# Four edits to a hand-made planner: shorter keep-up products, another issuer for one copy, a longer order search, another load order

## The chip, the cores and the metric

The kernel runs on one core of one Trainium2 chip. A core has TensorE (PE) for matrix products, VectorE (DVE), ScalarE (ACT), GpSimd (POOL) and SyncE (SP), which here only issues transfers. Each engine carries out its own list of instructions in order and waits on semaphores for the others; transfers run on 16 DMA engines. The metric is the device time in microseconds of one execution.

## The reference

Blocked attention, then a layer of two matrix products with a gated softmax between them. The shapes are B=4, H=8, S=768, D=64; x has 3072 rows of 512; w_in is 512x1024, w_out 1024x512; all float32.

```
k_sum = k.reshape(B,H,24,32,D).max(axis=3)        # one key for each block of 32
v_sum = v.reshape(B,H,24,32,D).mean(axis=3)       # one value for each block
scores = [ scale*q@k.T where |i-j| < 16, else -1e9  |  scale*q@k_sum.T + log(32) ]
a   = softmax(scores);   attn = a @ [v | v_sum];   x = attn as rows of H*D
h   = x @ w_in
solu = h * softmax(h)
ln  = (solu - mean)/sqrt(var + 1e-6) * g_ln
out = ln @ w_out
```

## The kernel before

Rows of x are cut in 24 tiles t of 128. Each batch has 768 rows, in three groups g of 256 rows, and each group has two tiles. The window of 16 neighbours is taken by loading, for each 64 queries, the 96 keys and values around them (WIN); 24 block keys or block means follow, 120 columns in all (KC).

The work of a step, by the names of the profile:

- `scores` (L578): products of keys and queries into `s`. VectorE adds the mask and takes the row minimum of the negated score (L597), ScalarE takes exponentials (L605), and the sum's reciprocal scales them (L611, then L288/L289 on `e`).
- `values_turn` (L633, tile `t`): the weights are transposed on TensorE and copied by ScalarE or VectorE to `at` (L281 is the copy helper's ScalarE line, L282 VectorE's, L283 GpSimd's).
- `values` (L672, tile `x`): products with the values `vt`. Its copies are split in a high and a low part, `xh` and `xl` (L678), since each product with weights is made of three passes of reduced precision.
- `first(t)` (L697, tile `h`): 24 products with w_in. Then follow the maximum (L707), the exponential (L712), the product with h (L720) and the normalization (L723 to L745).
- `turn(t)` (L633, tile `lt`) and `second(t)` (L775, tile `o`): the transposed rows, 24 products with w_out; ScalarE scales and stores (L780, L784).
- weights arrive as 64-bit integers that hold float64 (`raw`, L356) and are rounded by shifts and masks on ScalarE, VectorE and GpSimd into a high and a low part (`rounded`, L368 to L388, then L281, L288/L289 or L400, L402); w_in comes in eight pieces of 512 KB, w_out in eight.

Block means of v: for batch 0 TensorE sums the rows `st_v` (three loads, L447, "r" in the load string) with a selector matrix (L459), and ScalarE copies the result to `vsum` (L463). The mean rows must stand below the window rows of every tile `vt`: `load_v2` (L541) copies them there with a transfer, after the tile's own load (`load_v`, L535). For the very first tile they are multiplied apart (L664). Batch 1's means are made the same way (L472) and brought to `vsum`, of which there is a single buffer, by four small transfers on ScalarE's queue (L485); batches 2 and 3 use GpSimd's sums (L501).

No order is written down. Every operation is declared with the engines that can do it, a cost for each, and what it reads and writes. `Plan.order` simulates the engines with these costs and gives every free engine the ready operation with the smallest due time; an operation that can run on several engines goes where it is cheapest then. `Plan.issue` computes due times, runs `order` with random noise added to them 64 times, keeps the order with the earliest planned end of TensorE's work, and emits the instructions in that order. So the lists of all engines, SyncE's loads included, follow the plan; SyncE's due time is its place in the program, plus the noise. The string LOADS gives the places of the first loads: k is a pair of heads' keys (400 KB), q half of the first queries (256 KB), w a piece of w_in (512 KB), r rows of v (512 KB), v the first tile of values (1024 KB), Q and V the second group's.

In gaps that the plan leaves on TensorE up to FILL = 80 us, `keep_up` puts products of zeros (L900) into a tile that is overwritten later, to keep TensorE's clock up; each counts as 0.22 us in the plan.

Of the kernel before, what the change touches and what calls it, by code (L numbers as in the profile page):

```python
# [43 lines left out]
WPT = 2  # L44


LOADS = "wwkwqkkkqwwwrrrwwvQV"
NEG = -8.0e9
SCALE = 1.0 / math.sqrt(D)

# [22 lines left out]
class Plan:  # L73
# [8 lines left out]
    START = 0.7  # L82
    COLD, FILL = 6.9, 80.0
    IDLE = 0.22
    WAIT, FAR = 1.5, 200
    DEAR = {"dve": 1.0, "act": 0.3, "pool": 1.0}
    SYNC = 0.13
    TRIES, NOISE = 64, 3.0

    def __init__(self):  # L90
        self.ops, self.rings, self.banks, self.idle = [], {}, {}, None
# [15 lines left out]
    def op(self, engine, cost, fn, r=(), w=(), nbytes=0, after=(), alt=(), port=False):  # L107

        deps = set(after)

        def of(table, part):
            for k, v in table.items():
                if part is None or k is None or k == part:
                    deps.update(v)

        o = Op({e: (c, f) for e, c, f in ((engine, cost, fn), *alt)}, deps,
               len(self.ops), nbytes, port)
        r = [x if isinstance(x, tuple) else (x, None) for x in r]  # L120
        w = [x if isinstance(x, tuple) else (x, None) for x in w]
        for b, part in r:
            of(b.writers, part)
        for b, part in w:
            of(b.writers, part)
            of(b.readers, part)
            for p in b.prev:
                deps.update(p.ops)
                p.gone = True
        assert not any(b.gone for b, _ in r + w)  # L130
        for b, part in r:
            b.readers.setdefault(part, []).append(o)
            b.ops.append(o)
        for b, part in w:
            b.writers.setdefault(part, []).append(o)
            b.ops.append(o)
        deps.discard(o)
        self.ops.append(o)
        return o

    def issue(self):

        for o in self.ops:
            for d in o.deps:
                d.users.append(o)
        for o in reversed(self.ops):
            o.due = min([u.due for u in o.users] + ([o.prio] if "pe" in o.can else []), default=o.prio)
            if "sp" in o.can:
                o.due = o.prio
        due, best = [o.due for o in self.ops], None  # L150
        for seed in range(self.TRIES):
            noise = random.Random(seed)
            for o, x in zip(self.ops, due):
                o.due = x + (noise.gauss(0.0, self.NOISE) if seed else 0.0)
            order = self.order()
            if order:
                end = max(o.end for o in order if "pe" in o.can)
                if best is None or end < best[0]:
                    best = end, order, [(o.start, o.end, o.engine, o.cost, o.fn) for o in self.ops]
        _, order, kept = best  # L160
        for o, x in zip(self.ops, kept):
            o.start, o.end, o.engine, o.cost, o.fn = x
        at, done = self.START, set()
        for o in order:
            if o.engine == "pe":
                while at + self.SYNC < min(o.start, self.FILL):
                    at += self.keep_up(at, done)
                at = max(at, o.start) + o.cost * (2 if o.start < self.COLD else 1)
            done.add(o)
            o.fn()  # L170
# [72 lines left out]
    def keep_up(self, at, done):  # L243


        for tag in "hxs":
            b = next((b for b in self.rings[tag] if b.ops[0] not in done), None)
            if b and all(o in done and o.end + self.SYNC < at for p in b.prev for o in p.ops):
                self.idle(b.ap)
                return self.IDLE * (2 if at < self.COLD else 1)  # L250
        return 0.1
# [3 lines left out]
def attn_then_solu(ctx: ExitStack, tc: tile.TileContext, q, k, v, vr, vb, w_in, w_out, g_ln, out):  # L255
# [3 lines left out]
    nc = tc.nc  # L259
    plan = Plan()  # L260
    op = plan.op
    pe, act, dve, pool, sp = "pe", "act", "dve", "pool", "sp"
# [274 lines left out]

    def load_v2(b, g):
        x, y = vt[b, g], vsum[b]
        e, cost, queue = (sp, 0.43, nc.sync) if b else (act, 0.8, nc.scalar)  # L540
        return op(e, cost, lambda: queue.dma_start(  # L541
            out=x.ap[WIN:KC], in_=y.ap[WIN:KC, :].rearrange("p (o c) -> p o c", o=1).broadcast_to([NB, G, DM])),
            r=[y], w=[(x, 1)], nbytes=NB * 8192)
# [254 lines left out]
    }  # L798
    for x in LOADS:
        first_loads[x].pop(0)()  # L800
# [8 lines left out]
    for i in range(2 * NKC):  # L809
        split_w_in(*divmod(i, 2))  # L810
        if i % 2 == 0 and i < 2 * NPP:
            run(values_turn(0, 0, i // 2))
            run(values(0, 0, i // 2, 0, True))

    begun = [load_v2(*its[1])]
    for i in range(3):
        load_v_rows(1, i)
# [20 lines left out]
    for t in range(NT):  # L838
        n, j = divmod(t, 2)
        b, g = its[n]  # L840
# [47 lines left out]
        if j == 1 and n + 2 < len(its):  # L888
            load_v2(*its[n + 2])
# [54 lines left out]
```

## Time and profile before

| | |
|---|---|
| median of 3 runs | 397.38 us (397.09 to 397.52) |
| profiled execution | 397.45 us |
| its span, first to last instruction | 395.7 us |
| mean granted TensorE clock | 0.999 |
| busy: PE, DVE, ACT, POOL | 386.6, 275.4, 248.7, 97.9 us |
| moved by transfers | 49.24 MB |

The span is what the views below divide up; 1.75 us of the execution's own time lie outside it. In a row of the timeline or of the chain of waits the first number is the start and the second the length. "SPq" and "ACTq" are instructions by which SyncE and ScalarE issue a transfer. Products on TensorE are pipelined and their ends are modelled, so that busy rows overlap. What stands in brackets at the end is idle time before the row and what ended it.

### The profile page before, as it was taken

What the parts mean: (1) busy time and instruction counts of PE and PEld (TensorE: products, weight loads), DVE (VectorE), ACT (ScalarE), POOL (GpSimd) and SP (SyncE); (2) the same over time, 40 slices, a digit from 0 to 9 for tenths busy, and PEclk for the clock granted to TensorE, in tenths of its full rate; (3) what the DMA queues carried; (4) which work ended last, traced back from release to release, by engine and by line L of the source; (5) the groups of instructions that cost most, each with busy time, mean ns of one, the idle gap of its engine ahead of it and who ended that gap; (6) DMA issues with size and microseconds to landing.
All of it is one profiled execution on the core that took longest, in us unless ns stands there. A gap on an engine that the chain in (4) does not pass through costs nothing.

```text
span 395.7 us, 9677 instructions
## 1 busy us (share of the span) xinstructions
PE 386.6 (98%) x3697; PEld 298.3 (75%) x3703; DVE 275.4 (70%) x884; ACT 248.7 (63%) x746; POOL 97.9 (25%) x245
## 2 busy tenths in 40 slices
PE   8999998999999999999999999999999999999996
PEld 3436766677878888878888888878888887878776
DVE  4999998999789866577767657657657654554330
ACT  3889686999798756658558466468466463533411
POOL 4224010416837221236220121221021021101100
PEclk9999999999999999999999999999999999999999
DMA  7999992136277320463330410430310000000011
GB/s 287 411 410 369 409 329 78 56 113 185 70 248 208 113 103 0 141 175 104 123 112 2 150 66 27 156 73 28 108 48 27 2 28 27 16 12 28 27 55 53
DMA packets 14994, 49.24 MB, mean 124 GB/s; under 512 B 1836, under 2 KB 2092, under 8 KB 13412
## 3 DMA queue, kind: packets, MB, share of 16 engines
q1 hardware_dynamic: 11084, 41.89, 30.8%
q10 hardware_dynamic: 3864, 6.74, 4.7%
q8 instruction: 29, 0.48, 0.5%
q14 instruction: 17, 0.14, 0.1%
HBM read 40.11 MB, written 6.29 MB: 117 GB/s over the span
## 4 chain that ended last, share of the span: by engine, by line
PE 85%; DMA 6%; ACT 3%; DVE 2%; issue 1%; ACTq 1%; SPq 1%; DVEq 0%
PE o L775 35%; PE h L697 30%; PE x L672 6%; PE s L578 5%; PE t L633 3%; PE lt L633 3%; DMA st_v<-in_vr 3%; DMA raw<-in_w_in 2%; DMA vt<-vsum 2%; PE vs_ps L459 1%; PE x L900 1%; ACT he L712 1%; DVE he L720 1%; ACT at L281 1%; PE x L664 1%
## 5 line engine op out<-in xcount | busy, mean ns | idle before, releaser
L775 PE MATMUL o<-w,lh 128*128 128x512 f32 (+1 forms) x400 | 128.0, 390 | 0.1
L697 PE MATMUL h<-w,xh 128*128 128x512 f32 x384 | 127.0, 398 | 0.4 <-DVE he L720 0.4
L605 ACT ACTIVATE e<-e,nm 128x120 f32<-128x120 f32 x192 | 73.1, 385 | 25.0 <-DVE nm L597 25.0
L775 PEld LDWEIGHTS o<-w,lh 128*128 128x128 f32 x400 | 74.1, 188 | 18.5 <-issue 2.4
L697 PEld LDWEIGHTS h<-w,xh 128*128 128x128 f32 x384 | 72.1, 188 | 18.9 <-ACT e L605 0.8
L775 PE MATMUL o<-w,ll 128*128 128x512 f32 (+1 forms) x200 | 76.9, 384 | 0.0
L697 PE MATMUL h<-w,xl 128*128 128x512 f32 x192 | 75.6, 394 | 0.0
L707 DVE TENSOR_REDUCE hm<-h 128x1 f32<-128x512 f32 x48 | 32.6, 686 | 42.7 <-PE h L697 42.7
L281 ACT COPY at<-t 120x512 f32<-120x512 f32 x46 | 24.8, 587 | 46.1 <-PE t L633 45.6
L775 PEld LDWEIGHTS o<-w,ll 128*128 128x128 f32 x200 | 37.6, 188 | 6.6
L697 PEld LDWEIGHTS h<-w,xl 128*128 128x128 f32 x192 | 36.1, 188 | 7.5
L597 DVE CUSTOM_DVE_ANT_0 e<-s,mask 128x120 f32<-128x120 f32 x192 | 40.6, 276 | 1.3 <-PE s L578 1.3
L712 ACT ACTIVATE he<-h,hm 128x512 f32<-128x512 f32 x48 | 32.8, 697 | 9.4 <-DVE hm L709 9.4
L605 ACT ACTIVATION_READ_ACCUMULATOR e<-e,nm 128x1 f32 x192 | 36.5, 190 | 0.0
L760 DVE TENSOR_TENSOR ll<-lt,lh 128x512 fp32r<-128x512 f32 x48 | 31.9, 682 | 6.0 <-ACT lh L281 5.8
L739 POOL TENSOR_SCALAR ss<-ss 128x1 f32<-128x1 f32 x24 | 7.1, 297 | 115.0 <-ACT sq L735 114.9
L720 DVE SCALAR_TENSOR_TENSOR he<-h,hz,he 128x512 f32<-128x512 f32 x48 | 34.1, 746 | 0.4
L672 PE MATMUL x<-at,vt 120*64 120x64 f32 (+1 forms) x768 | 28.3, 225 | 1.5 <-ACT at L281 1.5
L672 PEld LDWEIGHTS x<-at,vt 120*64 120x64 f32 (+1 forms) x768 | 24.6, 138 | 6.3 <-ACT at L281 2.8
L288 DVE TENSOR_TENSOR e<-e,z 128x960 f32<-128x960 f32 x23 | 26.6, 1156 | 0.5
L281 ACT CAST lh<-lt 128x512 fp32r<-128x512 f32 x33 | 18.6, 596 | 12.9 <-PE lt L633 10.0
L735 ACT ACTIVATE sq<-he 128x1024 bf16<-128x1024 f32 x24 | 25.2, 1050 | 0.2
(94 smaller groups left out, 499.6 us busy)
## 6 DMA issues: line engine op xcount, KB each, us to landing
vt<-in_v SPq DMA_DIRECT2D x12, 1024.0 KB, 5.4
kraw<-in_k SPq DMA_DIRECT2D x16, 400.0 KB, 9.1
out<-os ACTq DMA_DIRECT2D x23, 256.0 KB, 2.0
qt<-in_q SPq DMA_DIRECT2D x11, 512.0 KB, 5.5
raw<-in_w_in SPq DMA_DIRECT2D x8, 512.0 KB, 10.7
raw<-in_w_out SPq DMA_DIRECT2D x8, 512.0 KB, 9.5
st_v<-in_vr SPq DMA_DIRECT2D x6, 512.0 KB, 12.5
st_v<-in_vb SPq DMA_DIRECT2D x8, 384.0 KB, 3.3
```

What stands on the lines that cost most here:

```text
L281: by = {act: lambda: nc.scalar.copy(out=to(), in_=of()), dve: lambda: nc.vector.tensor_copy(out=to(), in_=of()), pool: lambda: nc.gpsimd.t ...
L288: by = {dve: lambda: nc.vector.tensor_tensor(out=to(), in0=a(), in1=b(), op=kind), pool: lambda: nc.gpsimd.tensor_tensor(out=to(), in0=a() ...
L597: nc.vector.tensor_tensor_reduce(out=e.ap[:, n, :], in0=sc.ap[:, j, (2 * i + up) * KC:(2 * i + up + 1) * KC], in1=mask[:, mi, :], scale=-S ...
L605: nc.scalar.activation(out=e.ap[:, n, :], in_=e.ap[:, n, :], func=AF.Exp, bias=nm.ap[:, n:n + 1], scale=-1.0, accum_out=z.ap[:, n:n + 1])
L672: nc.tensor.matmul(xp()[j * D:(j + 1) * D, i, qs], vs.ap[:k, u, cs], at.ap[:k, u % 2, n[j] + u // 2, :], start=not apart, stop=not apart o ...
L697: nc.tensor.matmul(hp.ap, a.ap[:, c, ts], w.ap[:, i], start=(c == 0 and n == 0), stop=(c == NKC - 1 and n == 2))
L707: op(dve, 0.6, lambda i=i, hp=hp: nc.vector.tensor_reduce(out=nms.ap[:, i:i + 1], in_=hp.ap, op=ALU.max, axis=AX.X, negate=True), r=[hp], ...
L712: op(act, 0.71, lambda i=i, hp=hp: nc.scalar.activation(out=part(i), in_=hp.ap, func=AF.Exp, bias=nm.ap, accum_out=zs.ap[:, i:i + 1]), r=[ ...
L720: op(dve, 0.67, lambda i=i, hp=hp: nc.vector.scalar_tensor_tensor(out=part(i), in0=hp.ap, scalar=zs.ap[:, 0:1], in1=part(i), op0=ALU.mult, ...
L735: op(act, 1.13, lambda: nc.scalar.activation(out=sq.ap, in_=e.ap, func=AF.Square, accum_out=ss.ap), r=[e], w=[sq, ss])
L760: op(dve, 0.6, lambda part=part, r=r: nc.vector.tensor_tensor(out=part(lo), in0=tp.ap[:, r], in1=part(hi).bitcast(F32), op=ALU.subtract), ...
L775: nc.tensor.matmul(o.ap[:, cols], a.ap[:, f, :], w.ap[:, i, cols], start=(f == 0 and n == 0), stop=(f == NFC - 1 and n == 2))
```

## The change

Four parts. The gap in front of a product is filled with zero products only to 0.6 us ahead of its planned start (EASE). The copy of the means for the third group of batch 0, tile (0, 2), is issued by SyncE, where ScalarE issued it; the second group's stays on ScalarE. The search makes 500 tries. The first 16 are as before, with noise of 10 where it was 3; each later one takes the noises of the best try so far and adds new noise to about two in a hundred operations. A try is kept when the planned end of TensorE's work plus half the mean end of its operations isn't later. And the load string is another.

```
-LOADS = "wwkwqkkkqwwwrrrwwvQV"
+LOADS = "wkwqkkwkqwwrwrrwwvQV"
...
+    EASE = 0.6
...
-    TRIES, NOISE = 64, 3.0
+    TRIES, NOISE = 500, 10.0
+    FIRST, FEW = 16, 0.02
...
-        due, best = [o.due for o in self.ops], None
-        for seed in range(self.TRIES):
-            noise = random.Random(seed)
-            for o, x in zip(self.ops, due):
-                o.due = x + (noise.gauss(0.0, self.NOISE) if seed else 0.0)
+        due, best, rnd = [o.due for o in self.ops], None, random.Random(0)
+        for i in range(self.TRIES):
+
+            noise = [x + (rnd.gauss(0.0, self.NOISE) if i < self.FIRST or rnd.random() < self.FEW else 0.0) * (i > 0)
+                     for x in (best[3] if i >= self.FIRST else [0.0] * len(due))]
+            for o, x, n in zip(self.ops, due, noise):
+                o.due = x + n
             order = self.order()
             if order:
-                end = max(o.end for o in order if "pe" in o.can)
-                if best is None or end < best[0]:
-                    best = end, order, [(o.start, o.end, o.engine, o.cost, o.fn) for o in self.ops]
-        _, order, kept = best
+                ends = [o.end for o in order if "pe" in o.can]
+                end = max(ends) + 0.5 * sum(ends) / len(ends)
+                if best is None or end <= best[0]:
+                    best = end, order, [(o.start, o.end, o.engine, o.cost, o.fn) for o in self.ops], noise
+        _, order, kept, _ = best
...
-                while at + self.SYNC < min(o.start, self.FILL):
+                while at + self.SYNC + self.EASE < min(o.start, self.FILL):
                     at += self.keep_up(at, done)
...
-        e, cost, queue = (sp, 0.43, nc.sync) if b else (act, 0.8, nc.scalar)
+        e, cost, queue = (sp, 0.43, nc.sync) if b or g > 1 else (act, 0.8, nc.scalar)
```

## The prediction

> **What bounds the kernel now.** I read the page first (busy shares, then the slices), next the chain of waits in order of time, then tables by stage, and last the timelines and transfers around the places that the diff touches.
>
> ```profile
> span 395.7 us, 9677 instructions
> PE 386.6 (98%) x3697; PEld 298.3 (75%) x3703; DVE 275.4 (70%) x884; ACT 248.7 (63%) x746; POOL 97.9 (25%) x245
> DVE  4999998999789866577767657657657654554330
> ```
>
> TensorE (PE) is busy 98% over the whole span, but VectorE (DVE) stands at eight or nine tenths only up to the tenth slice (99 us), apart from the first, and falls to three at the end. So there are two stages with different limits. The chain of waits shows where they part:
>
> ```profile
> 9.56 10.83 DMA st_v<-in_vr
> 23.02 1.83 PE x L900 x8
> 25.99 0.81 PE x L900 x3
> 26.80 3.55 PE vs_ps L459 x8
> 31.95 0.62 PE x L664 x4
> 34.53 1.46 PE h L900 x6
> 38.39 5.79 PE h L697 x24
> 53.50 6.18 DMA vt<-vsum
> 59.69 1.35 issue
> 61.04 0.72 ACTq L485
> 78.24 1.46 PE x L900 x6
> 80.34 0.75 PE x L900 x3
> 97.16 5.60 PE h L697 x24
> 392.65 0.47 ACT os L780
> ```
>
> The columns are start, length and what the chain passed through. From 97.16 to 392.65 us the chain is TensorE alone, 295.5 us without a hole, and none of that work is removed. Before 97 us it goes through transfers, keep-up products (L900), ScalarE and VectorE. Whatever the change is worth is won or lost in the first 97 us. What stands after 392.65 (the last scaling and store, 3.1 us) is untouched.
>
> The table by stage (length; then busy time and instructions of PE, PEld, DVE, ACT, POOL; clock; DMA share; GB/s):
>
> ```profile
> 4.76:20.00 15.24, 13.94 (x171) 7.18 (x172) 14.03 (x52) 11.08 (x30) 3.01 (x3) 1.00 1.03 406
> 20.00:38.40 18.40, 17.56 (x206) 8.48 (x208) 18.36 (x59) 16.24 (x57) 6.58 (x15) 1.00 1.03 395
> 38.40:60.00 21.60, 21.60 (x206) 15.64 (x207) 20.90 (x58) 16.75 (x52) 1.64 (x2) 1.00 1.02 363
> 60.00:75.00 15.00, 13.20 (x165) 9.89 (x163) 13.27 (x42) 11.73 (x29) 4.91 (x14) 1.00 0.25 75
> 75.00:97.20 22.20, 21.47 (x229) 15.45 (x223) 21.95 (x74) 21.42 (x64) 7.72 (x15) 1.00 0.39 119
> ```
>
> VectorE idles 1.21, 0.04, 0.70, 1.73 and 0.25 us in these stages, 3.9 us of 92.4. It is the real limit of the start: reaching the state of 97.2 us with the same VectorE work can come at most 3.9 us sooner, unless work moves to ScalarE (15.2 us idle there) or GpSimd (69 us idle). The transfer engines are full to 60 us. TensorE's busy time hides waste, since keep-up products count in it: after 60 us it idles 1.80 + 0.73 us and spends 1.46 + 0.75 us of the chain on products that compute nothing, 4.7 us in all.
>
> **The change part by part.** The profiled execution took 397.45 us, 1.75 us more than its span; the median of the runs is 397.38, so the sum against 397.45 is lowered by 0.07 at the end.
>
> *Load order.* The gate of the first tile's values is the mean of v, which needs the third load of rows ("r", st_v), and the last piece of w_in is the gate of its conversion. The rows below are SyncE's timeline (start, length, issue) and the transfers issued at 14.16 and 16.55 us (size, us to landing):
>
> ```profile
> 0.79 0.38 SPq L356 DMA_DIRECT2D raw<-in_w_in  x1
> 14.16 0.33 SPq L447 DMA_DIRECT2D st_v<-in_vr  x1
> 16.55 0.33 SPq L356 DMA_DIRECT2D raw<-in_w_in  x1
> st_v<-in_vr SPq DMA_DIRECT2D x1, 512.0 KB, 12.5
> raw<-in_w_in SPq DMA_DIRECT2D x1, 512.0 KB, 11.4
> ```
>
> The third r lands at 14.16 + 12.5 = 26.7 us, which is just when the eight mean products start (26.80). The last w lands at 16.55 + 11.4 = 27.95, so 512 KB take 1.3 us. SyncE's eighteen issues from the first of these rows to the third r (the second row) are, in order, w k q q k w w w k k w w Q r r w v r: not the old string, because the search's noise also moves loads. With 512 KB for w, r and Q, 400 for k, 256 for q and 1024 for v, 8768 KB pass up to the third r. By the new string they are 6720 KB, 2048 less, so at 1.3 us per 512 KB the third r lands 5.2 us earlier, near 21.5. The last w (7744 KB against 9280) lands 3.9 us earlier. The first v comes 8768 KB deep instead of 8256, 1.3 us later, near 26.7, and becomes the next gate: the first products with v and the means could start near 27 instead of 31.95. The first q lies one w deeper than in the timeline, which costs the first scores up to 1.3 us. So the gain at the gate is 5.2 us at the most, and the other end is a loss of 1.3. VectorE decides what is kept: it idles 1.25 us from 4.76 to 38.4, and has the eight w pieces, the maxima and the scores to do anyway. I take −1.5 us, close to that idle time, because an earlier landing cannot speed an engine that had no wait to lose; the rest would need conversions to be put ahead of later scores.
>
> *Products that keep the clock up (EASE 0.6).* A gap is now filled only to 0.73 us before its planned end instead of 0.13, so two or three products of 0.23 us (1.83 for eight) go from the end of each. Five runs of fills stand in the chain, 6.31 us together; the most that can come off is 5 x 0.6 = 3.0 us. It is no gain where the work behind wasn't ready: the three fills at 25.99 end within 0.1 us of the landing above. It is a gain where work had become ready in a part of the gap. I take −0.9 for three of the five at half of 0.6 each; the ends are 0 and −3.0. What covers the products' absence is only that the clock holds, which is a rival below.
>
> *SyncE issues the third group's means.* Tile (0,2)'s copy of the means goes from ScalarE's queue to SyncE's. ScalarE's timeline around it, what waited behind it, and SyncE's issues of the tile and of keys of batch 1, the last two of them with their time to landing:
>
> ```profile
> 52.99 1.08 ACT L281 COPY at<-t 120x512 f32<-120x512 f32 x2
> 53.50 0.81 ACTq L541 DMA_DIRECT2D vt<-vsum  x1
> 61.89 0.84 ACT L281 COPY kw<-kraw 128x768 f32<-128x768 f32 x1 [2.20 <-issue]
> PE x L672 <- ACT at L281: 1.5, 2, 1.0
> 42.70 0.39 SPq L535 DMA_DIRECT2D vt<-in_v  x1
> 43.82 5.20 SPq L430 DMA_DIRECT2D kraw<-in_k  x4
> kraw<-in_k SPq DMA_DIRECT2D x2, 400.0 KB, 10.2
> ```
>
> ScalarE had other work until 53.50, so the copy was issued late, and landed at 59.69. The rows of batch 1's means (L485) overwrite the buffer that it reads, and they are issued by ScalarE in order: it stood still for 2.2 us, and TensorE later waited 1.0 us in one piece for ScalarE's at. On SyncE the transfer can go as soon as its tile is loaded. The tile's load is issued at 42.70 us, and loads of that time take up to 10.2 us, so it can go near 53 at worst. The direct saving is ScalarE's issue slot, 0.81 us; at the chain it is at most the 1.35 us before 61.04. The price is that SyncE stands until that load has landed, with the key loads of batch 1 and later q and v behind it. I take −0.7, half of the latter end, since ScalarE is idle elsewhere in this stage; ends −1.4 and 0 where the keys are ahead of it, the loss is a rival. By the Trainium skill, "DMA: Bandwidth & Descriptors", section "Issuing engines are not separate DMA queues", transfers from any queue share the same engines, and changing the issuer saves the issue time alone; by that, this term would be bounded by the 0.81 us, and the sum would stay within 0.1 us.
>
> *Order searched in 500 steps.* The instructions and their count don't change, only their order, the choice among engines for those that have one, and when SyncE issues. The first 16 tries disturb every due time with 10 instead of 3; then two operations in a hundred are shifted and a try is kept when the planned end plus half the mean planned end of TensorE's operations isn't worse. The mean rewards early progress too. What it can still win on the chip is the 4.7 us after 60 less what the two terms above take out of it, and conversions moved off VectorE. I take −0.7 from it; −2.5 at best, about half of the 4.7, and at the other end +3.0, as large as the best of the fills, since an order that is better in the plan may be late in places where the trace shows full engines.
>
> Sum: −1.5 − 0.9 − 0.7 − 0.7 = −3.8, just inside VectorE's 3.9 us of idle time. 397.45 − 3.8 − 0.07 = 393.6 us.
>
> **The rivals.** *(A) VectorE keeps its pace and nothing moves.* Loads land earlier, but the engine behind them is full (18.36 of 18.40 us), and removed fills become idle time. For it: nothing of VectorE's work is taken away. Against: its 1.73 us idle at 60 to 75, just behind the means' copy. The time is 397.4, within 0.2% (0.8 us, about what a measurement of this kernel can tell from no change).
>
> *(B) SyncE stands in front of the keys, and it is slower.* The maximum over the block keys that uses one of the last key loads:
>
> ```profile
> 59.43 0.94 DVE L439 TENSOR_REDUCE ksum<-kraw 128x24 f32<-128x768 f32 x1
> ```
>
> The two last key loads, issued at 48 to 49 us, land near 59, and this maximum starts at 59.43: there is no slack. If the new order puts the copy of the means ahead of these loads and the tile lands at 52.9 (42.70 + 10.2), they are issued some 4 to 5 us later, and keys, scores and values follow. It decides from the point where the wait is longer than what the other three terms bring, 3.1 us: −3.1 + 5 = +1.9, 399.3 us. Against it: in the old order the four key issues were over at 49 us, ahead of that landing.
>
> *(C) The clock falls in an unfilled gap.* The weight loads of the first products show the slow state:
>
> ```profile
> 2.07 0.15 PEld L900 LDWEIGHTS <-zero 128*128 128x128 bf16 x1 [0.28 <-issue]
> 2.50 0.15 PEld L900 LDWEIGHTS <-zero 128*128 128x128 bf16 x1 [0.27 <-issue]
> 5.85 1.39 PEld L900 LDWEIGHTS <-zero 128*128 128x128 bf16 x7 [0.21 <-issue]
> ```
>
> The products come every 0.43 us until 5.85, then every 0.20, though the granted clock reads 1.00 throughout. From 1.24 to 5.85 us, 4.6 us ran at half pace, so one fall costs about 2.3 us of work. TensorE's longest wait in the trace, 1.0 us, plus 0.73 leaves 1.7 us, far from 4.6 of quiet. If two gaps fell, it would give −3.8 + 4.6 = +0.8, 398.2 us. The Trainium skill, "TensorE: Matmul & The Clock Gate", section "Part 1: The HAM clock gate (the "warmup" mystery)", puts the window of the clock's monitor at about 3.4 us, so that one fall would cost half of that, an estimate of 1.7 us; by that, two falls would leave −0.4 and the time at 397.0, and one gap of 1.7 us would be too short for any.
>
> *(D) The conversions overtake.* If the first tile's products (38.39) start near 34 because v is the only gate and GpSimd takes more of the conversions, the load term is −4.4, and the sum −6.7: 390.7 us.
>
> **How the numbers follow.** The forecast has 0.50, D 0.16, A 0.14, B 0.15, C 0.05. Forecast and D are faster: 0.66; A is the same: 0.14; B and C are slower: 0.20. The predicted time is the forecast's, 393.6 us; its own range is 391.5 to 396.5. For 8 in 10 the range goes below to 389.0, past D with some of the terms' far ends, and above to 398.5, through A and C and a part of B; outside lie about 0.05 below and 0.12 above.
>
> **What would show it.** Load order: the eight mean products (L459) start by 24 instead of 26.80, and the first tile's h products by 36.5. If the rows land earlier but h still starts near 38, VectorE took the gain. Fills: the runs of L900 in the chain (8, 3, 6, 6 and 3 products) shorter or gone, the weight loads of those that are left still 0.2 us apart. Means: ScalarE issues one copy of the means instead of two, its 2.2 us stand is under 1, and L485 starts before 60 us. Search: TensorE's last uninterrupted stretch begins earlier than 97.16 by the sum of the terms, and is as long as now. The prediction is wrong if that stretch begins at the same time with VectorE as full as before (A), if key maxima wait for transfers around 55 to 65 us (B), or if products after a gap are spaced 0.43 us (C).

## The result: 2.7% slower

The changed kernel takes 408.0 us (median of 6 runs, 405.63 to 409.11) against 397.24 for the kernel before in the same comparison: 1.0269 times as long (95% interval 1.0238 to 1.0300). The forecast was 393.6 us. The profiled execution took 407.34 us. One run of all those below, of 2091.63 us in b_search_al96, lies far outside and counts in no comparison. In the changed kernel every line from the planner's new constants on stands some six lines lower: L697 (`h`) is now L703, L775 (`o`) L781, L459 (the mean products) L465; in the kernels with fixed places further down, lines stand 12 to 16 lower again.

The page of the changed kernel: span, busy shares, and the slices of VectorE and of the granted clock.

```profile
span 405.6 us, 9616 instructions
...
PE 386.6 (95%) x3670; PEld 296.6 (73%) x3673; DVE 270.4 (67%) x865; ACT 255.5 (63%) x755; POOL 110.6 (27%) x255
...
DVE  3989899999888586477746657548567644635220
...
PEclk9997999999999999999999999999999999999999
```

TensorE is busy for exactly as long as before, 386.6 us, in a span 9.9 us longer. Two things are new: the clock's fourth slice is at 0.7, and VectorE, which before had a single eight from the second slice to the tenth, has two there. The tables by stage, first of the kernel before, then of the changed one (length; busy time and instructions of PE, PEld, DVE, ACT, POOL; clock; DMA share; GB/s):

```profile
0.00:60.00 60.00, 56.62 (x589) 32.62 (x595) 53.57 (x168) 45.35 (x138) 14.87 (x36) 1.00 0.98 368
60.00:97.00 37.00, 34.47 (x386) 25.16 (x386) 35.02 (x115) 32.95 (x89) 12.63 (x28) 1.00 0.33 101
97.00:390.00 293.00, 292.94 (x2706) 238.10 (x2705) 186.78 (x603) 169.45 (x518) 70.37 (x181) 1.00 0.24 79
```

```profile
0.00:60.00 60.00, 50.45 (x551) 30.25 (x557) 48.96 (x153) 43.50 (x128) 18.72 (x38) 0.94 0.95 357
60.00:97.00 37.00, 34.56 (x380) 25.06 (x377) 36.06 (x103) 33.73 (x97) 14.77 (x28) 1.00 0.29 94
97.00:390.00 293.00, 289.11 (x2668) 230.80 (x2660) 184.08 (x609) 174.87 (x529) 77.15 (x191) 1.00 0.24 80
```

The same of the changed kernel in two shorter stretches:

```profile
30.00:40.00 10.00, 8.20 (x117) 5.31 (x115) 9.63 (x43) 7.64 (x27) 2.94 (x3) 0.78 1.03 362
40.00:50.00 10.00, 10.00 (x52) 7.59 (x50) 8.66 (x16) 7.32 (x28) 3.52 (x2) 0.88 0.94 341
```

By 60 us VectorE has worked 4.6 us less than before (48.96 against 53.57). After 97 us TensorE, which stood still for 0.06 us before, stands still for 3.9 us and has 38 products fewer in its records of the same 293 us. Taking each product at its median price in the kernel before and following how far the real products have come, the changed kernel is 1.5 us behind at 97 us, 8.8 at 385 and 9.9 at its last product. **Most of the loss lies where the prediction said that nothing could be lost or won.**

What TensorE waited for after 97 us in the changed kernel (us in total, times, longest; the kernel before has no such row there):

```profile
PE h L703 <- DVE he L726: 1.8, 4, 1.3
PE t L639 <- POOL e L295: 0.6, 1, 0.6
PE o L781 <- DVE w L408: 0.6, 1, 0.6
PE s L584 <- DVE at L288: 0.3, 1, 0.3
PE o L781 <- DVE ll L766: 0.2, 1, 0.2
```

These are 3.5 of the 8.4 us that are lost after 97 us. About 1 us more, by the starts of the products, is lost at the steps from one kind of product to another beyond what these rows show: there are 33 steps from `o` to `h` where the kernel before has 16. A further part isn't idle time at all: the products themselves lie further apart. From their starts in the timeline, the mean distance from one product of 512 columns to the next of its kind is 233.2 ns after 97 us, and 230.9 in the kernel before; over a thousand products that is 2.3 us. The 1.6 us that are left of the 8.4 are not assigned. A row of busy time doesn't show it, since the modelled ends overlap (a product's row is 0.39 us long).

### The profile page after: what moved, and what is told of

The parts are those of the page before. It is cut to its first block, busy times and chain, and to the rows that moved or that the text cites. A ratio compares the mean times of both kernels' runs of the same rounds, so it can differ in the third digit from the quotient of the medians.

```text
span 405.6 us, 9616 instructions
## 1 busy us (share of the span) xinstructions
PE 386.6 (95%) x3670; PEld 296.6 (73%) x3673; DVE 270.4 (67%) x865; ACT 255.5 (63%) x755; POOL 110.6 (27%) x255
## 5 line engine op out<-in xcount | busy, mean ns | idle before, releaser
L703 PE MATMUL h<-w,xh 128*128 128x512 f32 x384 | 132.1, 404 | 3.8 <-DVE he L726 3.7
L781 PE MATMUL o<-w,lh 128*128 128x512 f32 (+1 forms) x400 | 132.1, 392 | 0.6 <-DVE w L408 0.6
L703 PEld LDWEIGHTS h<-w,xh 128*128 128x128 f32 x384 | 72.7, 189 | 25.6 <-DVE he L726 7.6
L781 PEld LDWEIGHTS o<-w,lh 128*128 128x128 f32 x400 | 74.1, 188 | 19.1 <-issue 2.2
L781 PE MATMUL o<-w,ll 128*128 128x512 f32 (+1 forms) x200 | 77.5, 387 | 0.2 <-DVE ll L766 0.2
L703 PE MATMUL h<-w,xl 128*128 128x512 f32 x192 | 76.3, 398 | 0.0
L781 PEld LDWEIGHTS o<-w,ll 128*128 128x128 f32 x200 | 37.6, 188 | 8.5 <-DVE ll L766 1.2
L703 PEld LDWEIGHTS h<-w,xl 128*128 128x128 f32 x192 | 36.5, 190 | 7.8
L287 ACT COPY at<-t 120x512 f32<-120x512 f32 x43 | 23.3, 588 | 24.8 <-PE t L639 20.3
L611 ACT ACTIVATION_READ_ACCUMULATOR e<-e,nm 128x1 f32 x192 | 37.5, 195 | 0.0
L734 POOL TENSOR_SCALAR he<-he,nmu 128x512 f32<-128x512 f32 x15 | 15.6, 1043 | 70.8 <-DVE nmu L729 70.8
L786 ACT ACTIVATE os<-o,y 128x512 f32<-128x512 f32 (+1 forms) x22 | 14.7, 668 | 29.1 <-PE o L781 20.7
L678 PE MATMUL x<-at,vt 120*64 120x64 f32 (+1 forms) x768 | 29.2, 229 | 0.1
```

Of the source, the lines that this page charges most:

```text
L287: by = {act: lambda: nc.scalar.copy(out=to(), in_=of()), dve: lambda: nc.vector.tensor_copy(out=to(), in_=of()), pool: lambda: nc.gpsimd.t ...
L611: nc.scalar.activation(out=e.ap[:, n, :], in_=e.ap[:, n, :], func=AF.Exp, bias=nm.ap[:, n:n + 1], scale=-1.0, accum_out=z.ap[:, n:n + 1])
L678: nc.tensor.matmul(xp()[j * D:(j + 1) * D, i, qs], vs.ap[:k, u, cs], at.ap[:k, u % 2, n[j] + u // 2, :], start=not apart, stop=not apart o ...
L703: nc.tensor.matmul(hp.ap, a.ap[:, c, ts], w.ap[:, i], start=(c == 0 and n == 0), stop=(c == NKC - 1 and n == 2))
L734: op(pool, 0.62, lambda sl=sl: nc.gpsimd.tensor_scalar(out=e.ap[:, sl], in0=e.ap[:, sl], scalar1=nmu.ap, scalar2=1.0, op0=ALU.add, op1=ALU ...
L781: nc.tensor.matmul(o.ap[:, cols], a.ap[:, f, :], w.ap[:, i, cols], start=(f == 0 and n == 0), stop=(f == NFC - 1 and n == 2))
```

## The first two sets of experiments: parts of the change

Each comparison has its own runs of the kernel before (medians of 396.85 to 397.2 us). A kernel whose name begins with a starts from the changed kernel, one with b from the kernel before; all are one file with its parts switched. The first set takes the change apart.

**a_ease0**, the changed kernel with its own orders and the gaps filled to the end:

```
-    EASE = 0.6
+    EASE = 0.0
```

> The changed kernel with EASE = 0: the same order on every engine, gaps filled to 0.13 us before the planned start as in the kernel before. Theory 1 (the unfilled ends let the clock fall for one or two windows of 3.4 us at half pace): the granted clock is 0.999 again and the time drops by 3.4 to 4.5 us, to 403.5 to 404.6, with the rest of the loss still there. Theory 2 (the searched order has no slack and TensorE waits for other engines): the same drop, no more. Rival (the fills that are left out had stood in front of ready work): no drop, or a rise of up to 3 us.

406.41 us (1.0243, 1.0212 to 1.0273), 1.6 less than the changed kernel, where 3.4 to 4.5 had been expected; in the profiled run the clock is still at half from 37.3 us, but for 3.41 us, not 6.83. Between runs of one mean clock nothing is gained: 406.2 us here and 405.63 in the changed kernel at 0.996, 408.59 here and 407.34 and 407.60 there at 0.992. **b_ease** is the kernel before with EASE = 0.6 alone:

> The kernel before with EASE = 0.6 alone; its order is unchanged, 60 planned fills instead of 83. Theory 1 in its strong form: the clock falls here too, 1.7 to 3.4 us slower, 399 to 400.6. Theory 2: the fall needs the searched order's larger holes, so the clock stays at 0.999 and the time stays within 0.2% of 397.2. The prediction's step: 0.9 us faster, 396.3.

397.61 us, 1.0030 times (1.0011 to 1.0049). By itself the shorter filling brings nothing and costs a little. In the profiled run (397.59 us) the clock is at half for 3.41 us from 21.4 us on, but that isn't shown to be the reason: five of the six runs at 0.999 to 1.0 took 397.35 to 397.75, the sixth 400.84.

**a_oldsearch** is the changed kernel with the 64 attempts of before, so with loads, means and EASE:

```
-    TRIES, NOISE = 500, 10.0      (and the loop over them)
+    TRIES, NOISE = 64, 3.0
```

> The changed kernel with the old search (64 tries, noise 3, earliest end) and all else changed: load string, EASE, SyncE's copy. Theory 2: TensorE has no holes after 100 us again, and the time is within 1% of before, 394 to 400, depending on whether the clock falls. Rival theory 3 (the new load string and SyncE's copy make the start late): 402 or more, late before 100 us.

399.5 us (1.0060, 1.0037 to 1.0084). Here the load order does more than was forecast:

```profile
31.38 0.50 PE L700 MATMUL h<-w,xh 128*128 128x512 f32 x1
```

The first tile's product starts 7.0 us before the 38.39 of the kernel before, and yet the kernel is slower. **b_search** has the new search alone:

> The kernel before with the new search alone: old load string, ScalarE's copy, EASE = 0. Its plan ends 2.3 us earlier than that of before. Theory 2: TensorE waits after 100 us as in the changed kernel and the time is 402 to 405 with the clock at 0.999. Rival theory 3: no slower than before, 395 to 397.5, since loads and issuer are the old ones.

400.63 us (1.0100, 1.0074 to 1.0126), between the two forecasts, where its plan ends 2.3 us earlier. So one half of the change costs some 2.4 us, the other 4.0, and both 10.8.

The second set looked for the mechanism. **a_early** lets the noise act only on the first 600 of the 1624 operations:

```
-            noise = [x + (...) * (i > 0)
-                     for x in (...)]
+            noise = [x + (...) * (i > 0 and j < 600)
+                     for j, x in enumerate(...)]
```

> The changed kernel, with the search's noise on the first 600 of the 1624 operations only (those planned up to about 133 us); all later ones keep their due times. Its plan ends 0.3 us before that of the changed kernel, and has 15 changes from o to h products after 100 us where the changed kernel has 32. Theory 2 (the noise on the later operations mixes o and h products so that h starts the moment its bank is planned to be free, and every lateness becomes a hole): TensorE hardly waits after 100 us, the loss there is 23 to 25 us instead of 30, and the time is 400 to 403, the rest being the start and the clock. Rival (the holes after 100 us come from the late start alone): 406 or more.

401.81 us (1.0121, 1.0102 to 1.0141), in the profiled run with the clock at 1.0 up to the last product and 0.4 us of waits after 97 us: with the due times of the late part as they were, 6.2 of the 10.8 us are gone. **a_selq** builds the selector of batch 1's means with the first selector:

> The changed kernel with the same order, but the selector of batch 1's means (ten small GpSimd instructions, 2.76 us on the chip where the plan counts 0.8) is made in a tile of its own together with the first selector, near 5 to 8 us, when GpSimd has nothing else. Theory 3 (this one wrong price makes the tightly planned start late): the first h products start near 37.3 instead of 39.28 us, the clock falls for one window or none, and the time is 404 to 406. Rival (the start is late because of its loads): first h products within 0.5 us of 39.28, time 407 to 408.5.

405.02 us (1.0213, 1.0171 to 1.0254), within its forecast. But the trace doesn't bear out the reason given: the scores still start at 28.39 us (28.40 in the changed kernel), after 0.93 us of waiting, now for GpSimd's `cv`, and the first `h` at 38.53, where 37.3 was forecast and the changed kernel has 39.28. That profiled run took 407.59 us, with the clock at half for 6.83 us as in the changed kernel; the two runs at a clock of 1.0 took 404.21. So the 3 us seem to go with the clock for the most part. The selector in the changed kernel's start, on GpSimd and TensorE (start, length, instruction; in brackets the idle time before it):

```profile
25.84 0.18 POOL L344 MEMSET sel_q<- 128x96 f32 x1 [5.42 <-PE vs_ps L465]
...
28.41 0.19 POOL L351 TENSOR_SCALAR_AFFINE_SELECT sel_q<-sel_q 128x2 f32<-128x2 f32 x1
```

```profile
22.10 3.61 PE L465 MATMUL vs_ps<-st_v,sel 128*24 128x512 f32 x8 [1.62 <-DMA st_v<-in_vr]
...
28.40 1.05 PE L584 MATMUL s<-kw,qt 64*64 64x120 f32 x32 [1.04 <-POOL sel_q L348]
...
30.57 0.69 PE L678 MATMUL x<-at,vt 96*64 96x64 f32 x16
...
32.65 1.05 PE L584 MATMUL s<-kw,qt 64*64 64x120 f32 x32 [0.20 <-DVE nm L603]
35.30 0.90 PE L670 MATMUL x<-at,vsum 24*64 24x256 f32 x4 [1.60 <-DVE xl L684]
...
38.23 1.12 PE L678 MATMUL x<-at,vt 96*64 96x64 f32 x16
39.28 0.80 PE L703 MATMUL h<-w,xh 128*128 128x512 f32 x1
...
188.54 0.50 PE L703 MATMUL h<-w,xh 128*128 128x512 f32 x1 [1.28 <-DVE he L726]
```

The ten small instructions of the selector are planned at 0.8 us and take 2.76 (25.84 to 28.60). In the old order nothing waited for them. They were not the only gate, as a_selq shows. The sixteen products at 38.23 take 1.12 us, where the sixteen at 30.57 take 0.69: that is the half clock.

**a_hm** tests one long wait by itself. VectorE's minimum of two numbers took 1.19 us beside GpSimd's sums of 96x512, ahead of TensorE's wait of 1.28 us at 188.54; the same result comes from an instruction with one tensor operand:

```profile
182.56 1.19 DVE L715 TENSOR_TENSOR hm<-hm 128x1 f32<-128x1 f32 x1
```

```
-        nc.vector.tensor_tensor(out=nm, in0=nms[:, 0:1], in1=nms[:, 1:2], op=ALU.min)
+        nc.vector.tensor_scalar(out=nm, in0=nms[:, 0:1], scalar1=nms[:, 1:2], scalar2=None, op0=ALU.min)
```

> The changed kernel with the same order, but the minimum of the two halves' maxima (one column) is taken by an instruction with one tensor and a scalar operand instead of one with two tensors. In the changed kernel's trace this instruction takes 1.19 us at 182.56 and 0.80 at 121.15, against 0.16 usually, each time beside a GpSimd sum, and TensorE waits 1.44 and 0.76 us soon after. Theory 4 (GpSimd holds up an instruction that the plan prices at 0.07 us, and this makes the holes): these two holes go and the time falls by 1.5 to 2.2 us, to 405.8 to 406.5. Theory 2 alone: within 0.7 us of 408, as the holes open elsewhere.

406.81 us (1.0245, 1.0224 to 1.0266). That is a microsecond, short of what was expected, and 0.7 us between runs of nearly one clock (406.27 to 407.16 us at 0.991 to 0.992, against 407.34 and 407.60 at 0.992). The instruction now takes 0.22 us at the most, but TensorE's waits after 97 us come to 3.5 us again, so the holes opened elsewhere. **b_sp** moves the copy of the means alone, with the old search run anew over it:

```
-        e, cost, queue = (sp, 0.43, nc.sync) if b else (act, 0.8, nc.scalar)
+        e, cost, queue = (sp, 0.43, nc.sync) if b or g > 1 else (act, 0.8, nc.scalar)
```

> The kernel before with the one copy of the means on SyncE's queue and the old search over 64 seeds, which then picks another order (its plan ends 0.9 us earlier; 18 changes from o to h after 100 us). The prediction's step: 0.7 us faster, 396.5. Rival B of the prediction: keys wait behind the copy, 399 or more. Theory 2: with noise 3 the late part stays without holes, so within 1 us of 397.2 whatever the copy does.

402.65 us (1.0132, 1.0105 to 1.0159): one copy on another queue, and 5.2 us. A part of it is the copy's: in the profiled run (404.09 us) SyncE issues it at 54.60 us, later than ScalarE did, ScalarE's idle time where it issues the rows of batch 1's means is 3.24 us for 2.20 before, and TensorE waits 2.49 us in one piece for ScalarE's `at`. The rest, with products 232.8 ns apart where the kernel before has 230.9, made the orders themselves suspect, or something that changes with them.

## The third set: where the operands lie

Something does change with every order. A buffer gets its address when the first instruction that uses it is emitted, so each new order gives the buffers new places. The traces hold no addresses; those named here follow from the sizes of the buffers in the order in which they are given out. Sorted by the byte address of the stationary operand (`xh`, `xl`, `lh`, `ll`) over a multiple of 256, with all weights at 96, the spacings in the five traces compared fell apart cleanly: 227.4 to 227.8 ns where both parts lie at 96, 229.4 at 32, 233.3 at 64 and at 160. The edit that fixes places touches the buffers in a written order before the first instruction:

```
+PLACES = ("lh_0 ll_0 lh_1 ll_1 xh_0 xl_0 xh_1 xl_1 w0_0 sel_0 kraw_0 ...")
...
+        for x in PLACES.split():
+            self.pad(int(x)) if x.isdigit() else self.slots[x].ap
         at, done = self.START, set()
```

**a_lay** has in PLACES the order in which the kernel before touches them; **a_al96** and **b_al96** put the eight stationary buffers first, where they all begin at 96; **b_res** puts pads of 160, 128, 64 and 32 bytes ahead of the four pairs.

> The changed kernel with its own orders, but its tiles and banks given out in the order in which the kernel before first touches them, so that every buffer lies where it lies in the kernel before. Nothing else moves. Theory P (place): a product of 512 columns costs what the places of its operands make it cost; the changed kernel's 1127 such products lie 233.3 ns apart after 97 us and those of the kernel before 230.5, so 1127 x 2.8 ns = 3.2 us come back: 404.8 us (404.2 to 405.4), and the spacing after 97 us is 230 to 231 ns. Rival I (interleaving): the products are further apart because this order switches more often between the two kinds of product; then the spacing stays at 233 ns and the time at 408.0 (within 1.0).

> The changed kernel with its own orders, but the eight buffers of the stationary operands (lh, ll, xh, xl) given out first, so that each begins at 96 bytes over a multiple of 256, as every piece of the weights does. In all traces so far, products whose stationary operands begin at 96 lie 227.4 to 227.8 ns apart, at 32 229.4, at 64 or 160 233.3. Theory P: nearly all spacings go to 227.5: 1127 x 5.8 ns = 6.5 us, so 401.5 us (400.5 to 402.5). Rival I: no change, 408.0 (within 1.0). A middle case, in which only the products of the o kind follow the place: half of it, 404.8.

> The kernel before with its own orders, loads, means and search, and the same placing of the eight stationary buffers at 96 over a multiple of 256. Theory P: 230.5 becomes 227.5 ns: 1127 x 3.0 = 3.4 us, so 393.9 us (393.2 to 394.6), ahead of both kernels. Rival I: 397.3 (within 0.4). What could take it back: the products after 97 us then run ahead of their data and wait, in which case the waits of TensorE after 97 us show it.

> The kernel before with its own orders, and the stationary buffers in four pairs at four other residues of 256: lh and ll of even tiles at 0, of odd tiles at 128, xh and xl of even groups at 192, of odd ones at 224. The weights stay at 96. Theory P1 (distance to the moving operand): only a residue equal to the moving operand's is fast, so each of the four pairs is at 229 ns or more, most at 233.3, and the time is 399 to 401. Theory P2 (alignment by itself, lines of 256 or 128 bytes): the pairs at 0 and 128 are as fast as 96 or faster, at most 227.5, and the time is 394 to 397. Either way the mean of six spacings in one pair stays within 1.5 ns.

a_lay 407.0 us (1.0239, 1.0199 to 1.0279), a_al96 402.73 (1.0138, 1.0100 to 1.0176), b_al96 393.96 (0.9914, 0.9882 to 0.9946), b_res 399.28 (1.0043, 1.0023 to 1.0063). The last two lie within their forecasts; a_al96 is 1.2 us above the middle of its own and 0.2 outside it. Four rows of the chain in the kernel before, the same stretch of b_al96, of b_res and of b_m0 (below); 24 products each, an `o` row with 0.2 us for the step to the next kind:

```profile
209.33 5.75 PE o L775 x24
215.08 5.60 PE h L697 x24
...
223.86 5.66 PE o L775 x24
229.52 5.49 PE h L697 x24
```

```profile
207.06 5.67 PE o L790 x24
212.73 5.44 PE h L712 x24
...
221.34 5.67 PE o L790 x24
227.01 5.44 PE h L712 x24
```

```profile
210.13 5.79 PE o L790 x24
215.92 5.61 PE h L712 x24
...
224.71 5.79 PE o L790 x24
```

```profile
209.13 5.67 PE o L791 x24
214.80 5.49 PE h L713 x24
...
223.48 5.81 PE o L791 x24
229.29 5.60 PE h L713 x24
```

In b_al96 all but two of the full `h` rows after 100 us are 5.44 us (226.7 ns a product); in b_res, at 0, 128, 192 and 224 with the weights at 96, none of the four pairs is fast (232.7 to 234.2 ns). **b_m0** moves the weights to 0 and puts the four pairs at 0, 96, 192 and 32:

> The kernel before with its own orders; all pieces of the weights, the moving operands, at 0 over a multiple of 256 in place of 96; lh and ll of even tiles at 0, of odd tiles at 96, xh and xl of even groups at 192, of odd ones at 32. Theory P1 (distance to the moving operand): o of even tiles 227.4 ns, o of odd tiles 233 to 234, h of even groups 229.4 (64 below, as 32 against 96), h of odd groups 233. Theory P3 (96 and 32 are good by themselves): o even 233.3, o odd 227.4, h even 234.2, h odd 229.4. The time is about 397.7 by both, so only the spacings tell.

397.36 us in one run. `o` of even tiles, stationary at 0 as the weights, about 228 ns; of odd tiles, at 96, 234.3; `h` of even groups, 64 bytes below the weights, 229.0; of odd ones, 32 above, 233.1. So it isn't the address that counts but its difference to the moving operand, modulo 256: some 227 to 228 ns at 0, 229.0 to 229.4 at 192, and 232.7 to 234.3 at 32, 64, 96, 128, 160 and 224. Theory P1 stands; 96 isn't good by itself. Why the chip does so, no run here shows.

a_lay is the miss of this set: 1.0 us came off where 3.2 were expected. Three of its four runs have a clock of 0.987, so the medians hide a part; between runs of one clock it is 1.7 us (405.68 against 407.34 and 407.60 at 0.992; 406.86 to 407.48 against 408.39 to 409.11 at 0.986 to 0.987). The spacing went where theory P put it, from 233.2 to 231.1 ns after 97 us, but 2.1 ns a product were to be had and not 2.8, and the waits of TensorE grew from 3.5 to 3.9 us: so a part of the time saved in products seems to be spent in waiting for the same late data.

## The last two sets: the parts in equal places

> The changed kernel with the search of before (64 attempts, spread 3.0), so that it has the new loads, SyncE's means and EASE, and the eight stationary buffers at 96 over a multiple of 256. With the places of its own it took 399.5 us at 232.6 ns a product. Theory P: 1127 x (232.6 - 227.4) ns = 5.9 us come off: 393.6 (392.8 to 394.6), level with the kernel before in the same places (393.96), so that loads, means and EASE together are worth nothing either way, and its 399.5 was placement alone. Rival S (start): these parts cost about 2 us by themselves, and it stays at 395.5 or more.

> The kernel before with the new search alone (500 attempts, spread 10.0, the mean of the ends counted), in the same places. With its own places it took 400.63 us at about 231.9 ns a product. Theory P with slack: 5.1 us come off by the places, 395.5 (394.8 to 396.5), so that the searched order by itself costs 1.5 us against the kernel before in the same places, in waits of TensorE after 97 us. Rival: the search gains what its plan says (2.3 us) once the places are equal: 391.7.

> The changed kernel whose search puts its noise on the first 600 operations alone, in the same places. With its own places it took 401.81 us at 233.2 ns. Theory P: 1127 x 5.8 ns = 6.5 us come off: 395.3 (394.4 to 396.4); the 7.4 us between it and the changed kernel in the same places (402.73) are then the waits after 97 us and the half clock at 37 us, neither of which is in it. Rival C (clock): the half clock alone makes the 402.73, and it falls here too: 400 or more.

| | own places | stationary as the weights | plan's end |
|---|---|---|---|
| before | 397.24 | 393.96 (0.9914, 0.9882 to 0.9946) | 395.02 |
| loads, means, EASE (a_oldsearch) | 399.5 | 393.57 (0.9918, 0.9898 to 0.9937) | 394.17 |
| search alone (b_search) | 400.63 | 396.25 (0.9985, 0.9971 to 0.9999) | 392.71 |
| all, noise on 600 operations (a_early) | 401.81 | 396.17 (0.9979, 0.9965 to 0.9992) | 393.65 |
| all (the changed kernel) | 408.0 | 402.73 (1.0138, 1.0100 to 1.0176) | 393.92 |

All times are in us, ratios to the kernel before as it is. The first forecast was met; the other two came out 0.75 and 0.9 us above their middle, within their bounds. In equal places loads, means and EASE together are worth nothing that can be measured, and the 2.3 us that they cost before were placement. No run has the load string or the copy alone in equal places. The new search alone costs 2.3 us, the whole change 8.8. The plan's end (the kernel's own count, in the last column) doesn't order the five as the chip does.

Why does a searched order lose? TensorE's waits after 97 us in a_al96, then in b_al96:

```profile
PE h L715 <- DVE he L738: 1.5, 3, 0.9
PE t L651 <- POOL e L307: 1.1, 1, 1.1
PE s L596 <- DVE at L300: 0.4, 1, 0.4
PE s L596 <- issue: 0.4, 2, 0.2
PE s L596 <- DVE ll L778: 0.3, 1, 0.3
PE o L793 <- DVE ll L778: 0.2, 1, 0.2
PE t L651 <- DVE hm L727: 0.2, 1, 0.2
PE x L690 <- ACT at L299: 0.2, 1, 0.2
```

```profile
PE t L648 <- DVE e L303: 0.2, 1, 0.2
```

The last set asks whether the start or the thin plan makes them. **a_sync_al96** changes one number of the plan, **a_start_al96** keeps the order, builds the selector early and fills the gaps to their end:

```
-    SYNC = 0.13
+    SYNC = 0.3
```

```
-    op(pool, 0.8, selector, w=[sel_b])
+    op(pool, 0.8, lambda: (selector(), build_q()), w=[sel_b])    (and EASE = 0)
```

> The changed kernel in the same places (stationary buffers at the residue of the weights), with one number of its plan changed before the search: an operation may begin 0.3 us, not 0.13, after an operation of another engine on which it depends. In the trace of the changed kernel the steps between engines are longer than the plan's: the subtraction into ll takes 685 ns and 600 are planned, that into he 748 and 84 against 670, the minimum in hm 265 against 70. Theory L (no slack): an order searched with longer steps leaves room, TensorE's waits after 97 us fall below 1 us in all, and the time is 394 to 397 against 402.73, although the plan ends 2.0 us later (395.94 against 393.92). Rival S (the start): the order after 97 us isn't what costs; the time follows the planned end, 402.7 + 2.0 = 404.7, or stays at 402.7.

> The changed kernel in the same relative places (weights and stationary buffers all at 224 over a multiple of 256, since one small tile more lies ahead of them), with its own order; the selector of the third group's means is built right behind the other selector instead of between two waits, and EASE is 0, so that the gaps of the start are filled to their end. Rival S (the start): with the first products in time and no half clock, what was lost by 97 us (2.7) and much of the 6.6 us behind it come back, 396 to 399. Theory L: only the start comes back, 1.5 to 3 us, so 399.7 to 401.2, and the waits after 97 us stay at 3 us or more. With the weights and the stationary operands at one residue that is neither 96 nor 0, products lie 226.7 to 227.4 ns apart here too.

a_sync_al96 takes 397.01 us (1.0010, 0.9984 to 1.0037), 5.7 less than a_al96 (5.1 by the two ratios), with this one row of waits after 97 us:

```profile
PE s L596 <- DVE at L300: 0.2, 1, 0.2
```

Its plan ends 2.0 us later and the chip is 5.7 us faster, with a mean clock of 0.991 in both. By the count of real products used above, b_al96 is 1.2 us ahead of the kernel before at 97 us and 4.5 at 385; a_al96 is 1.6 behind at 97 and 4.9 at 385; a_sync_al96 is 1.7 behind at 97 and 0.7 ahead at 385. From the same standing at 97 us, then, a_al96 loses 6.6 us more on b_al96 and a_sync_al96 1.0. By that count b_search_al96 loses its time behind 97 us too, 2.7 us. a_start_al96 takes 400.44 us (1.0087, 1.0074 to 1.0100): 2.3 us come back, its waits after 97 us stay at 4.3 us in all. Theory L (no slack) holds on both counts (397.01 at the very end of its 394 to 397), but for one order of each kind: whether another draw of the search with the short step would lose as much as this one, no run shows. What stays open is how the 2.3 us divide between the selector and the clock: in the profiled run of a_start_al96 the clock was at half for 3.41 us from 23.4 us on, `h` started at 39.54 us (38.88 in a_al96), and the time was 403.12; its other five runs, at 0.999 to 1.0, took 399.93 to 400.50. So the gain shows only where the clock didn't fall.

**The sum.** Of the 10.8 us, 2.0 are the difference that places make (10.8 in the kernels' own, 8.8 in equal places; a_lay alone gives 1.0, or 1.7 at one clock). Of the 8.8, 2.3 go with the start and its half clock (a_start_al96). The 6.5 that are left belong to the order; 5.7 went when the plan had longer steps (a_sync_al96, whose start differs too, but which is as far behind at 97 us).

**A version that beats both kernels:** loads, means, EASE, the old search, and the stationary buffers placed as the weights: 393.57 us, 0.9918 times the kernel before. The kernel before with the places alone is as good within the intervals.

## Why the prediction was wrong, point by point

- *"Whatever the change is worth is won or lost in the first 97 us."* This step failed first. It read an unbroken chain of TensorE as work that can't be lost. The chain says that nothing was late in that order; it says nothing of how much later it could be, nor of what one product costs. 8.4 of 9.9 us were lost behind it.
- *Load order, −1.5.* The rows came as forecast: the eight mean products start at 22.10 us ("by 24"). But `h` started at 39.28, not by 36.5: the selector, `xl` and the half clock stood ahead of it. In a_oldsearch `h` starts at 31.38, more than was hoped, and in equal places the gain of the three parts together is 0.4 us, inside the intervals. There (a_oldsearch_al96), by the count of real products, 2.8 us are ahead of b_al96 at 42 us and none at 97. VectorE took most of them back, which was rival A's mechanism: it is busy for 36.66 of the 37 us from 60 to 97, and of TensorE's waits between 42 and 97 us, 2.6 us are for VectorE and 1.2 for ScalarE. By these runs the term should have been zero.
- *VectorE as "the real limit of the start"* held only for the old order. In the changed kernel it has 11.0 us idle by 60 us, where before it had 6.4: the order left it waiting.
- *EASE, −0.9.* No gain by itself (b_ease, 1.0030 times), 1.6 us of loss in the changed kernel (a_ease0), and between runs of one clock none. Half of rival C came true, the clock did fall (0.78 and 0.88 above), but it had been argued that a gap of 1.7 us is far from 4.6 us of quiet. From 35.6 us the clock was at half, and in the 3.4 us before that TensorE's timeline has two waits, 0.20 and 1.60 us, and 32 products of 64x120 between them: half a window of quiet was enough here. In a_ease0 it fell at 37.3 us after a single wait of 0.85 us in the 3.4 us before, while the 1.62 us ahead of 22.10 in the changed kernel were followed by no fall. So the waits alone don't tell when it falls.
- *SyncE's copy, −0.7.* It can go no sooner than its tile lands, and was issued later than ScalarE's 53.50:

```profile
46.16 3.27 SPq L436 DMA_DIRECT2D kraw<-in_k  x4
...
54.97 0.97 SPq L547 DMA_DIRECT2D vt<-vsum  x1
```

```profile
62.98 2.82 ACTq L491 DMA_DIRECT2D vsum<-vs  x4
65.86 0.68 ACT L374 ACTIVATE cv<-raw 128x512 f32<-128x512 f32 x1 [2.06 <-DMA vsum<-vs]
```

  ScalarE's idle time there is 2.06 us for 2.20, but it isn't the same stand. Before, ScalarE waited 1.35 us ahead of the first of the four issues at 61.04; now the four are issued in one piece, and the 2.06 us are time in which it issues. They start at 62.98, behind other work, and not before 60 as forecast, so that the term brought nothing that can be seen. In b_sp the idle time grew to 3.24 us. Rival B was wrong too: the key loads had all been issued (by 49.43) ahead of the copy.
- *Search, −0.7, with +3.0 at the far end.* This is the term that was mis-sized: +2.3 by itself in equal places, about +6.5 in the company of the other parts. Its far end was taken from the fills in the start, when nothing bounded what a thin order loses in 300 us. And the sum had no term for the buffers' places, which moved with the order and cost 2.0 us more.
- The Trainium skill, "TensorE: Matmul & The Clock Gate", section "Part 1: The HAM clock gate (the "warmup" mystery)", gives the clock's window as about 3.4 us; the traces agree, with falls of 3.41 and 6.83 us. The runs of the changed kernel show what a window costs: 405.63 us at a mean clock of 0.996, 407.34 and 407.60 at 0.992, 408.39 to 409.11 at 0.986 to 0.987, so 1.7 to 2.0 us for the second window (with one run at 0.996), near the prediction's estimate of 1.7 by that page. What the prediction drew from the window besides, that "one gap of 1.7 us would be too short for any", isn't borne out: the fall at 35.6 us came after 1.80 us of waits in two pieces.

## What to carry to other kernels

An engine that is busy without a hole can still be slowed down: compare the starts of equal instructions, not their busy time, before a new order is credited or blamed, and pin the buffers' places, or every reordering measures an address lottery as well (3 to 6 us in 400 here). An order found by search takes all the slack that its cost table shows; give the table the steps between engines as long as the trace has them: here the planned end came 2.0 us later and the real one 5.7 us earlier. A gain at the start counts only when the next full engine can use it.

## What the hardware did that was not expected

- A product of 512 columns took 226.7 to 234.3 ns from start to start at a full clock, by the difference of its two operands' byte addresses modulo 256: equal is best, in `h` and in `o`, with the weights at 96, 0 or 224 (a_start_al96: 227.7 and 228.1 ns on average after 97 us).
- The clock went to half for whole windows of 3.41 us, in the changed kernel after waits of 1.8 us in all, in a_ease0 after 0.85 us.
- A VectorE instruction with two operands of one number per row took up to 1.19 us beside GpSimd's sums (1.28 and 1.26 us, at 181.08 and 182.47); with one tensor operand none of the 24 took over 0.22 us (a_hm). Its row by tile in the changed kernel gives the shortest, the median and the longest in ns:

```profile
L715 DVE TENSOR_TENSOR hm<-hm x24: 145/160/1194, 47.3 to 371.9; 128x1 f32<-128x1 f32 x24
```
